# Eight GpSimd-issued transfers of x into a scratch tile, beside the loads of up and w_down

## The chip, the cores and the metric

The kernel runs on one core of one Trainium2 chip. The metric is the device time of a run in microseconds (us). Before the change the median of three runs is 411.18 us, with 411.07 and 411.40 at the ends.

A core has five engines that run their own instruction streams: TensorE (PE; its weight loads are shown as PEld), VectorE (DVE), ScalarE (ACT), GpSimd (POOL) and SyncE (SP). SP, ACT and POOL can issue transfers between the chip's memory (HBM) and the core's working memory (SBUF). A transfer is cut into packets, and these run on the core's 16 DMA engines. Each transfer counts up a semaphore as its parts land; instructions that need the data wait for the count.

## What is computed

One token is decoded through an attention block with a key and value cache and through a gated feed-forward block. Cut to what matters:

```python
# x (1,1,1024); k_cache, v_cache (1,4,65536,128); wq (1024,4096); wo (4096,1024)
# w_gate, w_up (1024,3584); w_down (3584,1024); all bf16
q = layernorm(x) @ wq                     # 32 heads of 128, 8 for each of the 4 cached heads
p = softmax(q @ k.T * 128**-0.5)          # over 65536 positions
h = x + (p @ v) @ wo
n = layernorm(h)
h2 = h + (gelu(n @ w_gate) * (n @ w_up)) @ w_down
```

Nearly all of the work is reading: 173.02 MB of weights and cache pass through the core once.

## The kernel before

**The ring and the order of loads.** All large inputs go through one SBUF buffer, `ring`, of four slots; `chunk()` hands out the next slot or slots. SP issues every large load in program order: wq (line 100), the cache (line 236, in `load`), wo (line 399), gate and up (line 441, in `ffn_in`) and w_down (line 497). A load waits until the matmuls (or, for k, the transposes) that read the slot's former contents are done. SP also issues ten small transfers (`c_dma`, line 395) of single rows of w_down into a tile `c_sb`, two after each large load from wo on.

**Attention.** For each of the four cached heads, `k_chunk` transposes k on DVE into tiles of the pool `ktpool` (tag "kt", six buffers) and multiplies on PE (line 257); the softmax runs on DVE and ACT; `v_chunk` multiplies the probabilities with v (line 306). The tail of this part multiplies with wo (line 404) and makes `h_col`, the columns of h (line 419).

**The feed-forward part.** `layernorm_cols` normalises h; GpSimd computes one step of it (line 159). `ffn_in` is called for gate and then for up: two loads each, 64 matmuls each (line 177), and a transpose of the result on DVE into a "kt" tile (line 189). Between the two calls the kernel prepares what the last product needs:

- `d_ps`, the accumulator of the output, is set to zero, and h is added into it by matmuls (line 472) that read the tile `hb`. GpSimd makes `hb`: a memset (line 467) and four copies from `h_col` (line 469).
- `actz`, a zeroed tile for the gated activations, is set by GpSimd (line 476); after up, DVE writes the activations into it (line 478).

Then `down` multiplies with w_down (line 484), which comes in four loads of 4096, 1792, 768 and 256 KB, and the result is copied (line 505) and stored by two transfers, one issued by SP (line 507) and one by ACT (line 508).

**What sets the order.** A scheduling layer records the operations and puts them into each engine's stream, with waits on semaphores between engines; a tile of a pool is given a buffer in turn, and its first writer waits for the last user of that buffer. At the end of the program SP waits for the completion counts of all transfers, two counts in an instruction, and then all engines meet in a barrier (the profile gives these instructions line 534). GpSimd issues no transfer in the kernel before.

Of the kernel before, what the change touches and what calls it, by code (L numbers as in the profile page):

```python
# [11 lines left out]
BF16 = mybir.dt.bfloat16  # L12
# [5 lines left out]
def kernel(  # L18
# [13 lines left out]
    nc = tc.nc  # L32
    P = 128
    D = A_x.shape[-1]
# [31 lines left out]
    ktpool = ctx.enter_context(tc.tile_pool(name="ktpool", bufs=6))  # L66
# [9 lines left out]
    def chunk(n=1):  # L76

        s0 = next_slot[0]
        assert s0 + n <= NSL
        next_slot[0] = (s0 + n) % NSL  # L80
        return ring[:, s0 * CW:(s0 + n) * CW]
# [91 lines left out]
    def wide_rows(banks, rows_z, ci, blocks, first, last):  # L173

        for t, w in enumerate(blocks):
            q = t % 4
            nc.tensor.matmul(banks[t // 4][32 * q:32 * q + 32, :], lhsT=rows_z[:, ci, :], rhs=w, start=first, stop=last,  # L177
                             tile_position=(0, 32 * q))

    def bank_pair(name, widths):  # L180
        return [ps_qk.tile([P, w], F32, name=name, tag="qk") for w in widths]

    def rows_to_columns(banks, name):

        w = [ps.shape[-1] for ps in banks]
        r = ktpool.tile([P, sum(w)], F32, name=name, tag="kt")
        o = 0
        for ps, n in zip(banks, w):
            nc.vector.transpose(out=r[:, o:o + n], in_=ps[:])  # L189
            o += n  # L190
        return r[:, 0:o:32]
# [200 lines left out]
    def c_dma():  # L392
        for _ in range(2):
            dst, src = c_loads.pop(0)
            nc.sync.dma_start(out=dst, in_=src)
# [32 lines left out]
    def f_blocks(w_row):  # L428

        blocks = []  # L430
        for o, n in zip((0, P * FA), FW):
            blocks += [w_row[:, o + q * n:o + (q + 1) * n].rearrange("k (j e) -> k e j", j=32) for q in range(4)]
        return blocks

    def ffn_in(wmat, name):
        banks = bank_pair(name + "_w", FW)
        wv_all = wmat.rearrange("(t p c) n -> t p c n", p=P, c=C4)
        for t in range(DS):
            w_sb = chunk()
            wv = w_sb[:, 0:C4 * F].rearrange("p (c n) -> p c n", c=C4)  # L440
            nc.sync.dma_start(out=wv, in_=wv_all[t])
            c_dma()
            for cc in range(C4):
                ci = t * C4 + cc
                wide_rows(banks, hz, ci, f_blocks(wv[:, cc, :]), ci == 0, ci == DC - 1)
        return rows_to_columns(banks, name + "_r")
# [21 lines left out]
    for i in range(4):  # L468
        nc.gpsimd.tensor_copy(out=hb[32 * i:32 * (i + 1), :, orow[i]:P:64],
                              in_=h_col[32 * i:32 * (i + 1), :].rearrange("p (t c) -> p c t", c=C4))  # L470
# [3 lines left out]
    AZ = 31  # L474
    actz = ptpool.tile([P, FC, 2 * AZ + 2], BF16, name="actz", tag="pt")
    nc.gpsimd.memset(actz[:], 0.0)
    u_r = ffn_in(B_w_up, "u_ps")
    nc.vector.tensor_tensor(out=actz[:, :, AZ], in0=u_r, in1=gl[:], op=ALU.mult)

# [59 lines left out]
```

## Time and profile before

| What | Value |
|---|---|
| Median of three runs | 411.18 us (411.07 to 411.40) |
| The profiled execution | 410.94 us, its span 409.0 us |
| Read from HBM | 173.02 MB, 423 GB/s over the span |
| PE busy | 243.9 us (60% of the span) |
| DVE busy | 204.7 us (50%) |
| ACT busy | 36.3 us (9%) |
| POOL busy | 35.9 us (9%), 119 instructions |
| Chain that ended last, by share | DMA 68%, DVE 22%, PE 5% |

The span runs from the first to the last instruction of the program in the profiled execution; the time of that execution is 1.94 us longer than the span. The profile page also cuts the span into 40 slices of 10.2 us and gives each engine's busy tenths; the chain of work that ended last is followed back from the last instruction, at each step to what released it. In the page's groups and in the timeline a line reads: engine, source line, operation, output<-input, shape and number.

The places named by their time are these: the last value loads are waited for from 288 us on, the wo product starts at 355.20 us, `h_col` is ready at 363 us, the gate product runs from 366.60 us, the up product in two halves from 380.75 and 389.27 us, the w_down product from 399.24 us, and the last store is issued at 406.67 us.

### The profile page before, as it was taken

What the parts mean: (1) busy time and instruction counts of PE and PEld (TensorE: products, weight loads), DVE (VectorE), ACT (ScalarE), POOL (GpSimd) and SP (SyncE); (2) the same over time, 40 slices, a digit from 0 to 9 for tenths busy, and PEclk for the clock granted to TensorE, in tenths of its full rate; (3) what the DMA queues carried; (4) which work ended last, traced back from release to release, by engine and by line L of the source; (5) the groups of instructions that cost most, each with busy time, mean ns of one, the idle gap of its engine ahead of it and who ended that gap; (6) DMA issues with size and microseconds to landing.
All of it is one profiled execution on the core that took longest, in us unless ns stands there. A gap on an engine that the chain in (4) does not pass through costs nothing.

```text
span 409.0 us, 3954 instructions
## 1 busy us (share of the span) xinstructions
PE 243.9 (60%) x1625; PEld 98.2 (24%) x1625; DVE 204.7 (50%) x262; ACT 36.3 (9%) x135; POOL 35.9 (9%) x119
## 2 busy tenths in 40 slices
PE   1337677688387457845765674677461423269865
PEld 1112222232132222311222221222130112131115
DVE  2118999999299339905980795099500000010210
ACT  1000000070000620000008000000340000000000
POOL 8223000300000400000002100000100100010000
PEclk9956988989889688866996888668885658588988
DMA  8999999999999999999999999999999999999995
GB/s 359 410 458 413 439 433 421 445 415 445 423 453 429 411 441 458 423 404 431 469 417 418 433 465 394 428 468 429 436 412 462 429 429 425 404 434 425 436 411 210
DMA packets 5441, 173.26 MB, mean 424 GB/s; under 512 B 688, under 2 KB 688, under 8 KB 1072
## 3 DMA queue, kind: packets, MB, share of 16 engines
q1 hardware_dynamic: 5368, 173.02, 98.4%
q8 instruction: 12, 0.20, 0.2%
q14 instruction: 5, 0.04, 0.0%
q10 hardware_dynamic: 56, 0.00, 0.0%
HBM read 173.02 MB, written 0.00 MB: 423 GB/s over the span
## 4 chain that ended last, share of the span: by engine, by line
DMA 68%; DVE 22%; PE 5%; issue 4%; SPq 0%
DMA ring<-in_A_k_cache_dram 42%; DVE kt L253 20%; DMA ring<-in_A_wo_dram 8%; DMA ring<-in_A_v_cache_dram 7%; DMA ring<-in_B_w_down_dram 6%; DMA ring<-in_B_w_up_dram 5%; PE qk_ps L257 2%; PE acc_ps L306 2%; DVE sc L267 1%; DVE mx L268 1%; PE at_ps L404 1%; SPq L100 0%; SPq L497 0%; PE d_ps L484 0%; DVE h L505 0%
## 5 line engine op out<-in xcount | busy, mean ns | idle before, releaser
L257 PE MATMUL qk_ps<-kt,qs 128*128 128x512 bf16 x512 | 141.3, 427 | 59.9 <-DVE kt L253 56.7
L253 DVE STREAM_TRANSPOSE kt<-ring 128x1024 f32<-128x1024 f32 x128 | 146.1, 1207 | 46.8 <-DMA ring<-in_A_k_cache_dram 46.8
L257 PEld LDWEIGHTS <-qs 128*128 128x128 bf16 x512 | 53.6, 105 | 144.4 <-issue 95.4
L306 PE MATMUL acc_ps<-ring,pt 128*32 128x512 bf16 x512 | 43.9, 519 | 48.2 <-DMA ring<-in_A_v_cache_dram 48.2
L290 ACT ACTIVATE pt<-sc,nbias 128x256 bf16<-128x256 f32 x64 | 31.5, 494 | 263.2 <-DVE nbias L283 263.2
L306 PEld LDWEIGHTS <-pt 128*32 128x32 bf16 x512 | 18.2, 126 | 72.3 <-issue 48.8
L324 DVE TENSOR_TENSOR oT_all<-o_ps,rl 128x8 bf16<-128x8 f32 x4 | 0.7, 167 | 45.1 <-PE o_ps L322 45.1
L267 DVE STREAM_TRANSPOSE sc<-qk_ps 128x512 f32<-128x512 f32 x32 | 22.1, 691 | 1.1 <-PE qk_ps L257 1.1
L268 DVE TENSOR_REDUCE mx<-sc 128x8 f32<-128x512 f32 x32 | 22.0, 688 | 1.1
L212 POOL MEMSET qs<- 128x2048 bf16 x4 | 7.2, 1804 | 94.5 <-PE qk_ps L257 94.5
L177 PEld LDWEIGHTS <-xz 128*32 128x32 bf16 x192 | 6.7, 123 | 35.1 <-issue 30.5
L177 PE MATMUL u_ps_w<-ring,xz 128*32 128x512 bf16 (+1 forms) x64 | 13.1, 974 | 2.2 <-DMA ring<-in_B_w_up_dram 2.2
L177 PE MATMUL g_ps_w<-ring,xz 128*32 128x512 bf16 (+1 forms) x64 | 12.9, 976 | 1.4 <-DVE xz L160 1.4
L404 PE MATMUL at_ps<-ring,o2z 128*32 128x512 bf16 x64 | 5.2, 493 | 12.6 <-DMA ring<-in_A_wo_dram 12.6
L216 POOL COPY qs<-qsel 32x32 bf16<-32x32 bf16 x64 | 11.2, 248 | 16.2 <-DVE qsel L207 15.5
L177 PE MATMUL qw_ps<-ring,xz 128*32 128x512 bf16 x64 | 7.2, 626 | 8.9 <-DMA ring<-in_A_wq_dram 8.9
L314 DVE TENSOR_TENSOR lsum<-lpart 128x8 f32<-128x8 f32 x4 | 0.7, 164 | 22.9 <-ACT pt L290 22.9
L290 ACT ACTIVATION_READ_ACCUMULATOR pt<-sc,nbias 128x1 f32 x64 | 12.0, 187 | 0.0
L419 DVE TENSOR_TENSOR h_col<-hc_ps,x_col 128x8 f32<-128x8 f32 x1 | 0.2, 167 | 20.3 <-PE hc_ps L412 20.3
L189 DVE STREAM_TRANSPOSE u_ps_r<-u_ps_w 128x512 f32<-128x512 f32 (+1 forms) x2 | 1.3, 650 | 13.8 <-PE u_ps_w L177 13.8
L189 DVE STREAM_TRANSPOSE q_r<-qw_ps 128x512 f32<-128x512 f32 x2 | 1.3, 696 | 13.1 <-PE qw_ps L177 13.1
L189 DVE STREAM_TRANSPOSE g_ps_r<-g_ps_w 128x512 f32<-128x512 f32 (+1 forms) x2 | 1.2, 650 | 12.4 <-PE g_ps_w L177 12.4
(94 smaller groups left out, 77.1 us busy)
## 6 DMA issues: line engine op xcount, KB each, us to landing
ring<-in_A_k_cache_dram SPq DMA_DIRECT2D x16, 4096.0 KB
ring<-in_A_wq_dram SPq DMA_DIRECT2D x2, 4096.0 KB
ring<-in_A_v_cache_dram SPq DMA_DIRECT2D x2, 4096.0 KB
ring<-in_B_w_gate_dram SPq DMA_DIRECT2D x2, 3584.0 KB
ring<-in_B_w_up_dram SPq DMA_DIRECT2D x2, 3584.0 KB
ring<-in_B_w_down_dram SPq DMA_DIRECT2D x1, 4096.0 KB
ring<-in_B_w_down_dram SPq DMA_DIRECT2D x1, 1792.0 KB
ring<-in_B_w_down_dram SPq DMA_DIRECT2D x1, 768.0 KB
```

The source lines that it names most:

```text
L177: nc.tensor.matmul(banks[t // 4][32 * q:32 * q + 32, :], lhsT=rows_z[:, ci, :], rhs=w, start=first, stop=last, tile_position=(0, 32 * q))
L189: nc.vector.transpose(out=r[:, o:o + n], in_=ps[:])
L212: nc.gpsimd.memset(qs[:], 0.0)
L216: nc.gpsimd.tensor_copy(out=qs[rows, :, s, SQ * i + s:SQ * (i + 1):NS], in_=qsel[rows, :, g * rep:(g + 1) * rep])
L253: nc.vector.transpose(out=kt[:], in_=k32[:, s * W:(s + 1) * W])
L257: nc.tensor.matmul(qk[:], lhsT=st["qs"][:, jt, s, :], rhs=mv[:, :, J, :, t], start=(s == 0 and jt == 0), stop=(s == NS - 1 and jt == 3))
L267: nc.vector.transpose(out=sc.rearrange("p n h s -> p (n h s)"), in_=qk[:])
L268: nc.vector.tensor_reduce(out=st["mx"][:, :, ci], in_=sc.rearrange("p n h s -> p h n s"), axis=AX.XY, op=ALU.max)
L290: nc.scalar.activation(out=pt[:].rearrange("p c n h s -> p (c n) h s")[:, :, r, :], in_=sc[:].rearrange("p c n h s -> p (c n) h s")[:, :, ...
L306: nc.tensor.matmul(acc[32 * c:32 * c + 32, :], lhsT=pt[:, ci % CPH, n, :, :].rearrange("p h s -> p (h s)"), rhs=v_sb[:, n:CH:NN, :], start ...
L314: nc.vector.tensor_tensor(out=lsum[:], in0=st["lpart"][:, 0, :], in1=st["lpart"][:, 1, :], op=ALU.add)
L404: nc.tensor.matmul(at_ps[32 * q:32 * q + 32, :], lhsT=o2z[:, c, :], rhs=wv[:, c, s * NB:(s + 1) * NB], start=(c < 2), stop=(c >= Hq - 2), ...
```

## The change

Between the zeroing of `actz` and the call of `ffn_in` for up, a scratch tile `marks` of 4 partitions x 8 x 256 elements (bf16) is taken from `ktpool`, and GpSimd issues eight transfers into it. Each reads all of x (1024 elements, 2 KB) as four rows of 256 elements, 512 bytes a row, into its own eighth of the tile. No instruction reads `marks`. The lines below the insertion are numbered five higher in the changed kernel.

```diff
     actz = ptpool.tile([P, FC, 2 * AZ + 2], BF16, name="actz", tag="pt")
     nc.gpsimd.memset(actz[:], 0.0)
+
+    NM = 8
+    marks = ktpool.tile([4, NM, D // 4], BF16, name="marks", tag="kt")
+    for i in range(NM):
+        nc.gpsimd.dma_start(out=marks[:, i, :], in_=A_x[0, 0].rearrange("(a b) -> a b", a=4))
     u_r = ffn_in(B_w_up, "u_ps")
     nc.vector.tensor_tensor(out=actz[:, :, AZ], in0=u_r, in1=gl[:], op=ALU.mult)
```

In the built program the first of the eight stands in GpSimd's stream between the memset of `hb` (line 467) and the copies into it (line 469); the other seven stand after those copies and are GpSimd's last work. None of the eight waits for a semaphore. On SP the closing waits become nine where there were five, since eight more completion counts are waited for; the count of SP's own output transfer stands in the second of the nine, where it stood in the third of the five. PE, DVE and ACT have the same instructions and waits as before.

## The prediction

> **What bounds the kernel now.** I read the page's DMA parts first, because the change adds transfers. In the second part of the page the DMA row gives, for 40 slices of the span, the busy share of the 16 DMA engines in tenths. In the third part the columns are packets, MB and the share of 16 engines' span.
>
> ```profile
> DMA  8999999999999999999999999999999999999995
> q1 hardware_dynamic: 5368, 173.02, 98.4%
> q8 instruction: 12, 0.20, 0.2%
> q14 instruction: 5, 0.04, 0.0%
> q10 hardware_dynamic: 56, 0.00, 0.0%
> ```
>
> The load queue (q1, issued by SP) fills the engines from the first slice to the last. q10 is the ACT queue (the load of x at line 95 and half of the output); q8 and q14 fetch instructions. Next, the end of the chain of work that ended last (start, duration, what):
>
> ```profile
> 358.42 22.29 DMA ring<-in_B_w_up_dram
> ...
> 381.22 24.73 DMA ring<-in_B_w_down_dram
> 405.96 0.04 issue
> 406.00 0.32 PE d_ps L484 x8
> 406.32 0.02 issue
> 406.34 0.29 DVE h L505
> ```
>
> The last 47 us are waits for loads; after the last load only 0.32 us of PE, 0.29 us of DVE, the two output transfers and the closing waits are left. In the trace's records of single DMA packets, joined end to start, every engine passes from one load packet to the next without a hole: the only holes over 0.2 us in 403 us are those in which an instruction fetch runs. So whatever engine time is added after 366 us delays the last load by as much, on the engines that finish last. How early the others finish is seen in the table of stretches (stretch, its length, busy time and instructions of PE, PEld, DVE, ACT, POOL, clock, DMA share, GB/s):
>
> ```profile
> 389.30:399.20 9.90, 6.78 (x36) 1.25 (x36) 1.74 (x4) 0.00 (x0) 0.00 (x0) 0.84 0.99 421
> 399.20:403.50 4.30, 4.04 (x160) 3.90 (x160) 0.00 (x0) 0.00 (x0) 0.00 (x0) 0.60 0.90 375
> 403.50:406.00 2.50, 1.49 (x81) 1.19 (x80) 0.00 (x0) 0.00 (x0) 0.00 (x0) 1.00 0.33 125
> ```
>
> The rate falls from 421 to 125 GB/s because engines run out of work one after the other. The 16 completions of the last load (256 KB of w_down) land from 402.72 to 405.96 us; the last five at 405.49, 405.66, 405.87, 405.93 and 405.96. A loss on an early engine is free up to its lead, at most 3.24 us; a loss shared by all is paid in full.
>
> **The change, part by part.** Nothing is removed. Added are eight transfers issued by GpSimd, each four rows of 512 bytes, 2 KB. No instruction reads `marks`, its "kt" buffer was freed long before, and in the built program PE, DVE and ACT keep the same instructions with the same waits. What differs is on POOL and SP.
>
> *POOL.* The first transfer stands between the memset of `hb` (L467) and the four copies into it (L469), the other seven after the copies. From the timeline:
>
> ```profile
> 365.98 0.53 POOL L467 MEMSET hb<- 128x512 f32 x1
> 366.57 0.89 POOL L469 COPY hb<-h_col 32x8 f32<-32x8 f32 x4
> ...
> 379.48 1.08 PE L472 MATMUL d_ps<-sel,hb 128*128 128x32 f32 x8
> ```
>
> The copies end at 367.46 and their reader starts at 379.48: 12.0 us of cover. No row shows a GpSimd issue. From below I bound it by an issue on SP (0.31 us, L507), from above by POOL's longest instruction (3.52 us, the memset of `c_sb`). Even at 3.52 us the copies end near 371 us, and all eight issues, 28.2 us, near 396 us, with nothing queued behind them until the program's end. Cost on POOL: 0 at both ends. If the first issue took over 12.0 us, the d_ps matmuls would be late, and past about 2 us more (PE waited 1.98 us for the second half of up at 389.27) the up matmuls too.
>
> *SP's closing waits.* SP closes the program by waiting for all completion counts, two in an instruction:
>
> ```profile
> L534 SPq EVENT_SEMAPHORE  x7: 17/28/889, 407.0 to 408.9; - x7
> ```
>
> Here the 889 ns one is the wait for SP's own output transfer, the third of five such waits; it ends at 408.05. The starts around it (407.03, 407.10, 407.17, then 408.09, 408.15, 408.22, 408.28) lie 61 to 69 ns apart. The built program has nine waits instead of five, and the one for that transfer is now second, so seven stand behind it where two stood: five more, 5 x 0.064 = 0.32 us, after the last transfer and hidden by nothing. I take +0.32; both ends are close (0.31 to 0.35).
>
> *Engine time of the added packets.* The nearest rows in kind and size are the ACT queue's load of the same x, early in the kernel beside full load traffic (the window from 3.6 to 6.5 us of the DMA view):
>
> ```profile
> q1 hardware_dynamic: 47, 1.54, 123.0%
> q10 hardware_dynamic: 47, 0.00, 0.9%
> ```
>
> In the packet records a 64-byte packet takes 8 to 11 ns, a 4-byte completion 9 ns, a 256-byte one 16 to 18 ns, and a 2,048-byte one 84 ns; along that line 512 bytes take about 27 ns. If the 32 rows are spread evenly, an engine gets two, 54 ns; with at most eight completions, 72 ns: 0.06 to 0.13 us per engine. I take 0.12.
>
> *Changing queues.* This is the unknown. In those rows a load packet of 32,768 bytes after a q10 packet takes 1,213 to 1,224 ns, as anywhere else (median 1,214): changing to ACT's queue and back costs nothing. From below, then, 0. The other rows of a foreign queue are the instruction fetches. A q14 packet of 8,192 bytes takes 309 to 325 ns, which is its bytes' time, but the load packet after it on that engine is longer by 312, 661, 380, 661 and 414 ns; after the q8 packets of 16,384 bytes (982 to 1,107 ns) it is longer by 467 to 550 ns. The size hardly matters, so I read it as a fixed price of 0.31 to 0.66 us, mean 0.49, for coming back from such a queue. From above, every visit costs 0.66 us. An engine gets between 2 visits (the rows alone, evenly spread) and 8 (each transfer touches every engine), so 0 to 5.3 us. The GpSimd queue is neither an SP nor an ACT queue; of the two I put a row-carrying visit nearest to the fetches, whose packets too come from another place of memory on a queue that neither SP nor ACT feeds, and a bare completion nearest to q10's 9 ns. Two visits x 0.49 = 0.98 us.
>
> The Trainium skill, page "DMA: Bandwidth & Descriptors", section "Why a DMA increments its semaphore by 16 and not by 1", says that a GpSimd-issued transfer has all 16 engines post a completion, whatever its shape; no row here shows it. By that rule each engine is visited eight times, and with the same return price the sum would be 8 x 0.49 + 0.32 + 0.12 = 4.4 us in place of the one below.
>
> **Sum.** 0.32 + 0.12 + 0.98 = 1.42 us (with 0.31 and 0.66 a visit: 1.06 to 1.76). The profiled execution took 410.94 us (span 409.0 and 1.94 us around it) and would become 412.36; the median of the runs is 411.18, so 412.6, its own range 412.2 to 412.9.
>
> **The rivals.**
> 1. *Hidden (not slower).* The visits cost as little as those to ACT's queue. Place: the load stream from 366 to about 396 us; price 0.12 us of packets plus 0.32 of closing waits; it decides if the return price is below 0.2 us (0.44 + 2 x 0.19 = 0.82 us is the bound of what can be told). For it: the q10 rows are the same source and nearly the same size, and the queue is read by the same engines. Against it: q10 is fed as SP's queue is, and the only rows of another kind all show a loss. Time 411.6.
> 2. *Every completion is a visit.* All 16 engines lose 0.31 to 0.66 us eight times: 2.5 to 5.3 us plus 0.44. For it: the price didn't depend on size. Against it: q10's completions cost 9 ns, and close visits could share one return. At 0.49: 415.5; at 0.31: 414.1. The rows all falling on the same four engines would come near it too, if those are among the last to finish; if they are early ones, their lead of up to 3.24 us takes it up.
> 3. *GpSimd's first transfer is slow and hb becomes late.* It decides above 14 us (12.0 of cover and 2 of PE's wait). No row on POOL is longer than 3.52 us. At 20 us: about 6 + 0.4, 417.6.
> 4. *Faster.* The fetches move with the instruction counts (POOL has eight transfers more), and one of them, 16,384 bytes at 403.57, lies in the tail. It occupies one engine for 1.07 us; but with completions at 405.93 and 405.96, freeing one engine gains 0.03 us alone. A gain of over 0.82 us would need several of the last engines relieved at once, up to 1.07 us: 410.1. I see no row for that.
>
> **How the numbers follow.** Forecast 0.37, hidden 0.30, every completion 0.23, slow first transfer 0.03, faster 0.07. About 0.2%, 0.82 us here, is what a measurement of this kernel can tell from no change; the forecast, the second and the third rival lie beyond it, slower 0.63; hidden is within it, 0.30; faster 0.07. The predicted time is the forecast's, 412.6. The range takes in the hidden case (411.6, less 0.2 for the spread of the runs before) and the second rival at 0.49 a visit: 411.4 to 415.5. Outside are the faster case, the slow first transfer and the dear end of the second rival.
>
> **What would show it.** In the new profile a further DMA queue stands with 32 rows and 32 to 128 completions, of about 9 and 27 ns. If the forecast holds, load packets of 28,672 bytes between 366 and 396 us that follow a row of the new queue take about 1.4 to 1.7 us instead of 1.07, two per engine, and the piece of w_down in the chain ends near 407.1. If rival 1 holds, none is longer and the last load lands near 406.1; if rival 2 does, some eight per engine are, and it lands near 410. L534 on SP should have eleven waits, seven of them behind that for the output, 0.45 us where two took 0.13. The copies into `hb` should end before 372 us; later than 379 would speak for rival 3. A new queue that makes the engines wait without longer packets, or a time around the span that differs from 1.94 us, would make the working wrong.

## The result, and the profile after

The changed kernel takes 411.76 us (median of 18 runs, 411.37 to 412.15) against 411.22 us (18 runs, 410.85 to 411.40) for the kernel before in the same measurement: ratio 1.0014, 95% interval 1.0008 to 1.0021. It is slower by 0.54 us. The interval lies above 1, and the difference below the 0.82 us that the prediction took as the bound and below the forecast's 1.42 us. The profiled execution took 411.37 us, its span 409.45 us.

The DMA parts of the changed kernel's page (busy tenths in 40 slices; queue, packets, MB, share of 16 engines):

```profile
DMA  8999999999999999999999998999999999999994
q1 hardware_dynamic: 5368, 173.02, 98.3%
q8 instruction: 12, 0.20, 0.2%
q0 software_dynamic: 256, 0.02, 0.0%
q14 instruction: 5, 0.04, 0.0%
q10 hardware_dynamic: 56, 0.00, 0.0%
```

q0 is the new queue. It carries 256 packets, not the 64 to 160 that were foreseen, and still takes 0.0% of the engines' time; the load queue keeps its packets, and the engines stay full. The end of the chain of waits of the changed kernel (start, duration, what):

```profile
358.09 22.94 DMA ring<-in_B_w_up_dram
...
381.54 24.67 DMA ring<-in_B_w_down_dram
406.21 0.04 issue
406.25 0.32 PE d_ps L489 x8
406.57 0.02 issue
406.60 0.29 DVE h L510
```

The path is the same. The last load lands at 406.21 us where it landed at 405.96, 0.25 later, and the two steps behind it are unchanged. The table of stretches of the changed kernel, with the columns of the one shown of before:

```profile
399.20:403.50 4.30, 3.77 (x160) 3.54 (x160) 0.00 (x0) 0.00 (x0) 0.00 (x0) 0.66 0.94 389
403.50:406.00 2.50, 1.34 (x80) 1.19 (x80) 0.00 (x0) 0.00 (x0) 0.00 (x0) 1.00 0.36 142
```

A little more traffic is left for the last 2.5 us: 142 GB/s instead of 125. In the records of completions, the last five of the last load come at 405.65, 405.71, 405.84, 405.86 and 406.21 us: four by 405.86, earlier than the last two before, and one engine alone late.

On GpSimd, the timeline of the changed kernel (start, duration, engine, line, operation):

```profile
365.73 0.52 POOL L467 MEMSET hb<- 128x512 f32 x1
366.20 0.71 POOL L481 DMA_DIRECT2D marks<-in_A_x_dram  x1
366.91 0.93 POOL L469 COPY hb<-h_col 32x8 f32<-32x8 f32 x4
367.77 3.58 POOL L481 DMA_DIRECT2D marks<-in_A_x_dram  x7
...
379.30 1.08 PE L472 MATMUL d_ps<-sel,hb 128*128 128x32 f32 x8
```

An issue costs GpSimd 0.52 us, the first 0.71. The copies into `hb` end at 367.84; their reader starts at 379.30. The rest of the view of the tile `marks` says when the data came:

```profile
L481 POOL DMA_DIRECT2D marks<-in_A_x_dram x8: 518/518/713, 366.2 to 370.8; - x8
...
DMA to landing us min/median/max: 6.6/11.0/15.8
```

The eight transfers of 2 KB took 6.6 to 15.8 us to land: they wait in the engines, not at GpSimd. Last, the closing line of the program, 539 now (engine, operation, count: shortest, median, longest ns, first and last start):

```profile
L539 SPq EVENT_SEMAPHORE  x11: 17/28/28, 407.3 to 409.4; - x11
...
L539 POOLq EVENT_SEMAPHORE_RANGE_CLEAR  x1: 139/139/139, 409.0 to 409.0; - x1
```

There are eleven waits where there were seven. SP's wait for its own output passes at 408.11 us; the seven behind it start at 408.18 to 408.55 us, 59 to 67 ns apart. Clearing the semaphores takes 139 ns where it took 96.

**The account of the profiled execution.** The last load is 0.25 us later. From the landing of SP's output to the end of the span it is 1.35 us instead of 0.95: +0.40, of which five more waits are 0.31 and GpSimd's longer drains and clearing about 0.07. SP's output itself landed in 1.18 us instead of 1.37: -0.19. The sum is 0.46, and the span grew by 0.47. The -0.19 does not go with the change: which of the two outputs lands first differs from profile to profile. SP's took 1.18 us in after and e5 and 1.19 in e8, where it was first, and 1.35 to 1.37 in before, e1, e4 and e6, where it was second.

### The profile page after: what moved, and what is told of

Same layout as the page of the kernel before. It is cut to its first block, busy times and chain, and to the rows that moved or that the text cites. A ratio compares the mean times of both kernels' runs of the same rounds, so it can differ in the third digit from the quotient of the medians.

```text
span 409.4 us, 3966 instructions
## 1 busy us (share of the span) xinstructions
PE 245.2 (60%) x1625; PEld 98.6 (24%) x1625; DVE 204.8 (50%) x262; ACT 36.3 (9%) x135; POOL 40.0 (10%) x127
## 4 chain that ended last, share of the span: by engine, by line
DMA 68%; DVE 22%; PE 5%; issue 4%; SPq 0%
DMA ring<-in_A_k_cache_dram 42%; DVE kt L253 19%; DMA ring<-in_A_wo_dram 8%; DMA ring<-in_A_v_cache_dram 7%; DMA ring<-in_B_w_down_dram 6%; DMA ring<-in_B_w_up_dram 6%; PE qk_ps L257 2%; PE acc_ps L306 1%; DVE sc L267 1%; DVE mx L268 1%; PE at_ps L404 1%; SPq L100 0%; SPq L502 0%; PE d_ps L489 0%; DVE h L510 0%
## 5 line engine op out<-in xcount | busy, mean ns | idle before, releaser
L257 PE MATMUL qk_ps<-kt,qs 128*128 128x512 bf16 x512 | 143.0, 432 | 57.5 <-DVE kt L253 48.6
```

Of the source, the lines that this page charges most:

```text
L257: nc.tensor.matmul(qk[:], lhsT=st["qs"][:, jt, s, :], rhs=mv[:, :, J, :, t], start=(s == 0 and jt == 0), stop=(s == NS - 1 and jt == 3))
```

## The experiments

Two questions stood open. How much of the 0.54 us is the closing waits and how much the load stream? And why did a foreign packet not cost what an instruction fetch costs: is it its size, its number, or the engines that it falls on? Differences below are against the runs of the kernel before that were taken with the experiment. For the endings, this table of profiled executions is used (us):

| Profile | last load lands | mean of its 16 completions | end of span | from the last landing to the end | median against before |
|---|---|---|---|---|---|
| before | 405.96 | 404.53 | 408.98 | 3.02 | |
| e8_shift_before | 405.97 | 404.51 | 408.96 | 2.99 | -0.17 |
| after | 406.21 | 404.69 | 409.45 | 3.24 | +0.54 |
| e5_after_again | 406.73 | 404.75 | 409.97 | 3.24 | +0.62 |
| e4_shift_after | 406.31 | 404.75 | 409.31 | 3.00 | +0.33 |
| e1_one32 | 406.35 | 404.70 | 409.49 | 3.14 | +0.37 |
| e6_late32 | 406.49 | 405.00 | 409.90 | 3.41 | +0.80 |

**The same kernel again (e5_after_again).** The changed kernel without an edit.

> The changed kernel as it is, timed on the same chip and against the same runs as the next three. Its profile had SP's closing waits and the clearing of counts at 0.38 us more than before, and all rows of the added transfers on four DMA engines, eight on each. Theory V (closing part 0.39; on those four engines eight rows of 27 ns and eight completions of 9 ns, 0.29): +0.4 to +0.7 us. If the first measurement was drawn low and the load stream loses as much as the runs with one transfer seemed to show (0.25 us on top): +0.8.

Measured 411.73 us (11 runs, 411.55 to 412.00) against 411.11: ratio 1.0014, interval 1.0005 to 1.0023. The 0.5 to 0.6 us stand. Its chain of waits:

```profile
382.05 24.69 DMA ring<-in_B_w_down_dram
406.73 0.04 issue
```

The load ends 0.52 us later than in the first profile of the same kernel, while the ending is 3.24 us in both. The last landing is the part that varies from one execution to the next (406.21, 406.31 and 406.73 us in the three profiles with these eight transfers), and a single profile can't place it better. The mean of the 16 completions is steadier: 404.53 and 404.51 us in the two profiles without the transfers, 404.69 to 404.75 in the three with them. By it the load stream loses 0.17 to 0.24 us on the average engine. The new queue's packets take 0.18 us an engine by their records.

**The closing waits moved (e4_shift_after, e8_shift_before).** One small load into `c_sb` is left out (8 of the 3,584 rows of w_down are then not multiplied). The counts are given out in turn, so both outputs move to the last two of them, and the other waits pass before the outputs land.

```diff
-    c_loads.append((c_sb[33:62:4, 2:3, :], c_views[3]))
...
-        for _ in range(2):
+        for _ in range(min(2, len(c_loads))):
```

e4 makes this edit in the changed kernel:

> The changed kernel without the last small load of w_down rows (8 rows of 2 KB; these 8 of the 3,584 rows of w_down are left out of the product), which shifts the completion counts by one: the two output transfers now use the last two counts waited for, so all other closing waits pass before the outputs land. Theory W: against the changed kernel 7 waits x 0.064 = 0.45 less and 0.09 less engine time: 411.76 - 0.54 = 411.2. If the closing waits cost nothing (the time is all lost in the load stream): 411.76 - 0.09 = 411.67.

Measured 411.38 us (411.07 to 411.72) against 411.05: +0.33, ratio 1.0008, interval 0.9999 to 1.0016. The closing line of this kernel:

```profile
L538 SPq EVENT_SEMAPHORE  x11: 17/28/28, 407.4 to 409.2; - x11
```

It still has eleven waits, but seven of them pass from 407.38 to 407.79 us, before the outputs land at 408.20 and 408.38. From the last landing to the end it is 0.93 us, as in the kernel before (0.95), and the ending of the table falls to 3.00. In the profile the waits cost by their place behind the outputs, not by their number. The median lies between the two cases named beforehand (no difference from the kernel before, or 0.45 us if the waits cost nothing), and its interval takes in both. e8 makes the same edit in the kernel before:

> The kernel before without the last small load of w_down rows (8 of the 3,584 rows are left out of the product), so that the two outputs use the last two completion counts waited for. Theory V: two waits less behind the output's landing, 0.13, and 0.09 us less on eight engines: -0.1 to -0.2 us, 410.9 to 411.0. It is the partner of the changed kernel with the same load left out: between the two only the engine time (0.29) and the longer clearing (0.07) remain, 0.36, where between the changed kernel and the one before there were 0.54.

Measured 410.94 us (410.55 to 411.27) against 411.11: -0.17, ratio 0.9994, interval 0.9985 to 1.0003; its ending is 2.99 us. So with the order of the closing waits equal, the eight transfers cost 0.33 + 0.17 = 0.50 us by the medians, where I had expected about 0.36, and with intervals of about 0.7 us on both medians the one is not told from the other. By the medians the shift is worth 0.21 to 0.29 us in the changed kernel and 0.17 in the kernel before, so the five added waits would come to 0.04 to 0.12 us; that neither confirms nor excludes the 0.31 of the profile. What is told apart is the ending: 3.24, 3.24 and (e6) 3.41 with seven waits behind the outputs, 3.00, 2.99, 3.02 without.

**One transfer instead of eight (e1_one32).** The same number of bytes in 32 rows, from wq, in one transfer: one count to wait for.

```diff
-    marks = ktpool.tile([4, NM, D // 4], BF16, name="marks", tag="kt")
-    for i in range(NM):
-        nc.gpsimd.dma_start(out=marks[:, i, :], in_=A_x[0, 0].rearrange("(a b) -> a b", a=4))
+    marks = ktpool.tile([32, D // 4], BF16, name="marks", tag="kt")
+    nc.gpsimd.dma_start(out=marks[:], in_=A_wq[0:32, 0:D // 4])
```

> One GpSimd transfer of 32 rows of 512 bytes (from wq) in place of eight of four rows: the same 16 KB and 32 rows, but one completion count instead of eight. Theory W (the 0.54 us is SP's closing waits, 0.32, the longer clearing of counts and drains on GpSimd at the end, 0.07, and 18 packets per engine, 14 of 9 ns and 2 of 27 ns, 0.18): here six closing waits with three behind the output's instead of two, 0.06, and two rows and a few completions per engine, 0.07 to 0.09: 411.22 + 0.15 = 411.37. Theory R (the rows themselves cost the load stream, 0.25 us each and two per engine): 411.7. Theory S (whatever it is, it is per transfer, 0.07 us each, in the load stream): 411.3. Load packets of 28,672 bytes stay at 1,066 ns under W and S, some are over 1,250 under R.

Measured 411.42 us (411.12 to 411.64) against 411.05: +0.37, ratio 1.0008, interval 0.9999 to 1.0017. From its page and from its chain:

```profile
q0 software_dynamic: 32, 0.02, 0.0%
```

```profile
381.66 24.69 DMA ring<-in_B_w_down_dram
406.35 0.04 issue
```

From SP's output to the end it is 1.08 us, 0.13 more than before: one more wait behind it (0.064) and GpSimd's part. The load stream did not get off free: the 32 packets are 16 of 1,024 bytes (two rows in one, 54 ns), one on every engine, and 16 of 4 bytes. The load packets behind the rows are longer by 0.05 to 0.09 us on all engines (one, on an engine that had just run an instruction fetch, by 0.41), neither unchanged nor over 1.25 us long, as the theories had it. Load packets that ran at that time without a row in front are longer too, by up to 0.07. In all that is about 0.085 us an engine, so each engine pays 0.054 + 0.085 + 0.009 = 0.15 us; the mean of the 16 completions is 0.17 later. 0.13 + 0.15 is 0.28 of the 0.37. I had left this lengthening out.

**Long rows (e3_rows8k, e7_spread8k).** If the price of a visit is fixed, rows of 8,192 bytes, the size of a q14 fetch, cost no more beyond their own time. e3 keeps eight transfers of four rows. The tile comes from the pool of `sc`, whose buffers are free earlier, so that GpSimd issues them at 298 to 305 us, beside the loads of v, whose packets are 65,536 bytes.

```diff
-    marks = ktpool.tile([4, NM, D // 4], BF16, name="marks", tag="kt")
+    marks = scpool.tile([4 * NM, HD], BF16, name="marks", tag="sc")
...
-        nc.gpsimd.dma_start(out=marks[:, i, :], in_=A_x[0, 0].rearrange("(a b) -> a b", a=4))
+        nc.gpsimd.dma_start(out=marks[4 * i:4 * i + 4, :], in_=A_wq[4 * i:4 * i + 4, :])
```

> The eight transfers with rows of 8,192 bytes (of wq) instead of 512, the size of the instruction fetches that made the next load packet 0.31 to 0.66 us longer. Theory W with price by bytes: two rows per engine at 0.31 us each instead of 0.027, so 0.57 us more than the changed kernel: 412.3. If the longer next packet comes with the size of a foreign packet (the price that the prediction put on a visit, but by size): 2 x 0.49 more, 413.3, and load packets behind such rows are 0.3 to 0.66 us longer in the trace. If it belongs to the fetch queues alone: 412.3 and no longer packets.

Measured 416.47 us (416.27 to 416.52) against 411.05: ratio 1.0129, interval 1.0114 to 1.0145. Its chain:

```profile
386.39 24.71 DMA ring<-in_B_w_down_dram
411.10 0.04 issue
```

That is 3 us above the dearest case named beforehand. The last load lands 5.14 us later than before, but the 16 completions of that load spread from 403.05 to 411.10 us: twelve come by 407.64, four from 409.93 on. In the packet records a row takes 0.32 us in the mean (309 to 512 ns) and the load packet behind it is longer by about 0.25 us in the mean (0.83 at most), and all 32 rows are on four engines, eight on each: 8 x (0.32 + 0.25) = 4.6 us there. The other twelve are late too: their completions have a mean of 405.23 us, against 404.53 for all 16 before. e7 spreads the same rows: two transfers of 16.

```diff
-    NM = 8
+    NM = 2
...
-        nc.gpsimd.dma_start(out=marks[4 * i:4 * i + 4, :], in_=A_wq[4 * i:4 * i + 4, :])
+        nc.gpsimd.dma_start(out=marks[16 * i:16 * i + 16, :], in_=A_wq[16 * i:16 * i + 16, :])
```

> The same 32 rows of 8,192 bytes as in the run with eight transfers of four rows, but in two transfers of 16 rows over 16 partitions, issued at the same place. Theory V (the four-row transfers put all their rows on the same four engines, eight rows each, 0.32 us a row and 0.24 on the next load packet, which is the 5.4 us of that run): with 16 rows a transfer every engine gets two rows: 2 x 0.56 = 1.1, closing part 0.2: +1.3 us, 412.4. If the cost comes with the bytes or rows in total, wherever they run: +5 us, 416. If a load packet behind such a row is longer by 0.49, the price of the prediction: 2 x 0.81 + 0.2 = 1.8.

Measured 414.18 us (414.00 to 414.63) against 411.11: ratio 1.0074, interval 1.0061 to 1.0086. Its chain:

```profile
384.54 24.75 DMA ring<-in_B_w_down_dram
409.28 0.04 issue
```

The place of the rows matters: two rows on every engine cost 2.3 us less than eight on four. But 16 such rows run at once, take 0.41 us each in the mean, and the load packet behind is longer by 0.75 us in the mean (0.08 to 1.2), so an engine pays 2 x (0.41 + 0.75) = 2.3 us on average, where I had counted with e3's price. The mean of the 16 completions is 3.04 us later than before, so 0.7 us stay outside this sum.

The packet records show where these 0.7 us lie, and they change the reading. Load packets that follow no row, but run while a row is read on another engine, are longer too: by 10 to 11 us in sum over the 16 engines in either kernel, 0.7 us an engine. In e7 the first row starts at 302.03 us, and nine load packets that had started 0.8 to 1.6 us earlier are already longer by 0.31 to 1.1 us. In the kernel before, only the load packets behind the two instruction fetches are long beside the loads of v. So the loss with these rows is not only a price on the packet behind: it falls on load packets of all engines. What causes it stays open. The rows of e1, e3 and e7 come from wq and those of the changed kernel and e6 from x, so the size of a row is not told apart from its source; e3 and e7 differ in how many rows run at once and on which engines.

**Four times as many transfers (e2_mid32, e6_late32).** To ask for a price by the transfer, 32 transfers of four 128-byte rows go into a constant tile in the middle of the cache loads.

```diff
+    NM = 32
+    marks = const.tile([P, 2, 64], BF16, name="marks")
+
+    def mark(i):
+        nc.gpsimd.dma_start(out=marks[4 * (i // 2):4 * (i // 2) + 4, i % 2, :],
+                            in_=A_x[0, 0].rearrange("(a b) -> a b", a=16)[0:4, :])
...
             k_chunk(g, ci)
+            if g == Hkv - 1 and ci == 0:
+                for i in range(NM):
+                    mark(i)
```

> 32 GpSimd transfers of four rows of 128 bytes of x, issued in the attention part after the last qs tile (about 140 us on) instead of eight in the tail; eight completion counts are used in turn, so the closing waits are nine as in the changed kernel. Theory W: closing waits 0.32, clearing 0.07, and 32 x 2 packets per engine of 9 ns (eight of them rows, some 12 ns): 0.60; together 0.99, 412.2. The engine time counts although it falls 150 us ahead of the end. Theory S (0.07 us per transfer in the load stream): 32 x 0.07 = 2.2, 413.5. If the place matters and time lost in the attention part is won back: 0.39, 411.6.

Measured 438.61 us (438.23 to 439.25): ratio 1.0671, interval 1.0656 to 1.0686, far from what was expected, and for a reason outside the question. Nothing in the program holds these transfers back, so the scheduler put them at the start of GpSimd's stream. Its timeline:

```profile
12.68 4.29 POOL L331 DMA_DIRECT2D marks<-in_A_x_dram  x8
20.45 0.52 POOL L331 DMA_DIRECT2D marks<-in_A_x_dram  x1 [3.48 <-DMA marks<-in_A_x_dram]
...
63.22 2.05 POOL L331 DMA_DIRECT2D marks<-in_A_x_dram  x4 [0.75 <-DMA marks<-in_A_x_dram]
65.27 5.91 POOL L216 COPY qs<-qsel 32x32 bf16<-32x32 bf16 x32
```

The first eight go out without a wait; the next twenty each wait for an earlier one to land, and the last four go out after one more wait (in brackets: the idle time before it and what ended it). GpSimd's transfers use eight completion counts in turn, so these are waits of the program for a count to be free. The copies into `qs` stand behind all of them and start at 65.27 us; in the kernel before they start at 28.27. The matmuls with the cache wait for them, and the loads for the matmuls:

```profile
PEld L257 <- POOL qs L216: 40.2, 2, 39.9
```

```profile
DMA  8999952698888999999999999999999999999995
```

The first is a line of the table of waits (40.2 us in two waits), the second the page's DMA row: the engines run dry in slices 6 to 8. This is the third rival's mechanism in a place without cover. e6 holds the transfers with a copy that writes `marks` from the last head's `qs`:

```diff
+                nc.gpsimd.tensor_copy(out=marks[:].rearrange("p a b -> p (a b)"), in_=kst[g]["qs"][:, 0, 0, :])
```

> 32 GpSimd transfers of four rows of 128 bytes, held back by a copy from the last qs tile, so that no work of the attention part stands behind them on GpSimd; eight completion counts in turn, nine closing waits. Theory V: closing part 0.39; the four engines with the rows get 32 x (13 + 9) ns = 0.70: 1.1 us in all, 412.2. Rows spread over all engines: 64 packets of 9 to 13 ns on each, 0.6: 1.0 us (not told apart by the time, but by the trace). If each visit made the next load packet longer, by 0.02 us on average as behind the 512-byte rows: 0.64 more on the four engines, 1.7 us. If time lost in the attention part is won back: 0.4.

Measured 411.91 us (411.66 to 412.18) against 411.11: +0.80, ratio 1.0018, interval 1.0010 to 1.0027. From its page and the view of its tile:

```profile
q0 software_dynamic: 1024, 0.02, 0.1%
```

```profile
L331 POOL DMA_DIRECT2D marks<-in_A_x_dram x32: 521/521/713, 139.3 to 214.7; - x32
...
DMA to landing us min/median/max: 6.8/21.9/27.9
```

That is under the 1.1 us expected. 32 transfers and 1,024 packets cost 0.2 us more than eight and 256, and SP's output to the end is 1.35 us as in the changed kernel. There is no price by the transfer worth naming: but for those that meet an instruction fetch, load packets behind a 128-byte row or behind 4 bytes are longer by less than 0.01 us in the mean.

## Why the prediction was right or wrong

**The direction and the range were right; the likeliest case was not the one that came.** The time is the first rival's: 411.6 foreseen, 411.76 measured, with its condition (a return price below 0.2 us) met. The forecast's own range, 412.2 to 412.9, missed; the stated range holds the time because it took in that rival.

**GpSimd: right.** Costed at nothing behind 12.0 us of cover. The first issue took 0.71 us of it and the other seven 3.58 us behind the copies. e2 shows what GpSimd's issues can cost without cover: 27.5 us for 32 of them and their waits.

**SP's closing waits: right by the profile.** Foreseen 0.32 us, seven waits behind the output taking 0.45; the trace has five more at 0.059 to 0.067 us, 0.31 in all, seven taking 0.435. GpSimd's drains and clearing, 0.07, were not in the sum. e4, where the same waits pass before the outputs land, has its ending back at 3.00 us; the medians are too wide to confirm it.

**Packet time: near, from wrong counts.** Foreseen 0.12 us on every engine, two rows and at most eight completions. In the joined records of load and q0 packets the rows were on four engines only, eight each, and every transfer put two packets on all 16 engines (a row and a completion, or two of 4 bytes). On the four engines that is 8 x 0.027 + 8 x 0.009 = 0.29 us, on the others 16 x 0.009 = 0.14.

**The return price: the step that failed.** The term "Two visits x 0.49 = 0.98 us" was mis-sized. A load packet behind a 512-byte row is longer by 0.014 us in the mean and 0.16 at most; behind 4 bytes, away from instruction fetches, by less than 0.005 in the mean. So two visits gave 0.03 us and eight on an engine 0.11, where 0.98 was foreseen. The step put the new queue nearest to the instruction fetches and read their loss as fixed, because 8,192 and 16,384 bytes cost alike; but the foreign packets at hand below that, q10's, had cost nothing. In the other runs the load packet behind was longer by about 0.07 us for 1,024 bytes, 0.25 for 8,192 on four engines and 0.75 for 8,192 on 16 at once. That size is the cause is not shown: those longer rows came from wq, and load packets without a row in front were longer beside them too. But a fixed price is excluded, and two sizes near each other do not show that size is without weight. Why an instruction fetch costs 0.31 to 0.66 us stays open. What is true of the step: not every visit is free. One of the four engines gathered 0.34 to 0.52 us of lengthening in each of the traces of after, e4 and e5, most of it behind rows and some behind 4 bytes (in after 38, 55, 62, 28, 61, 29, 87 and 159 ns). Whether this engine is the one that lands last is not shown, and why the other three have 0.1 us at most is open.

**The sum.** In place of 0.32 + 0.12 + 0.98 stand 0.2 to 0.4 for the ending (0.40 less what the output's landing happens to give back) and, by the mean of the completions, 0.17 to 0.24 for the load stream. Together that is 0.4 to 0.64, and 0.54 and 0.62 were measured. The last landing itself can't give the split: it varies by more than the term between two profiles of the same kernel.

**The rivals.** Every completion a visit fell: every engine had 16 packets of the new queue and not eight, and one of 4 bytes lengthened the next load packet by less than 0.005 us in the mean. Its last case, all rows on the same four engines, did come, but eight rows on an engine brought it 0.29 us of packets and 0.11 of lengthening in the mean, and not eight times 0.31 to 0.66. The slow first transfer fell for this place. Faster did not come: the lead of the early engines was there, but nothing relieved the last ones.

**The signs named beforehand.** 32 rows as foreseen, but 224 packets of 4 bytes instead of 32 to 128. No load packet behind a row is at 1.4 to 1.7 us (the longest is 1.07 + 0.16; those of 1.48 to 1.59 us in this stretch follow instruction fetches). The piece of w_down ended at 406.21, by the first rival's 406.1 and not the forecast's 407.1. The time around the span is 1.92 us.

## What to carry to other kernels

A few small transfers beside a saturated load stream cost here about their own packets on the engines that they fell on; ask which engines those are, and make their rows small or spread them, for rows of 8,192 bytes on four engines cost ten times as much (5.4 us), and spread over all of them 3.1. Each completion count that transfers use is also waited for at the end of the program, at 0.064 us for two counts, and in the profiles it costs only if the wait stands behind the last output's. And a transfer that nothing holds is put wherever the scheduler likes: look at what stands behind it on its engine, since in e2 and e6, after eight in flight, the issue itself waited for a landing.

## What the runs showed of the hardware that was not expected

- A GpSimd transfer of four rows puts two packets on each of the 16 engines: 32 packets per transfer, 256 in all. The Trainium skill, page "DMA: Bandwidth & Descriptors", section "Why a DMA increments its semaphore by 16 and not by 1", says that all 16 engines post a completion whatever the shape; the trace agrees.
- The rows of all eight transfers lie on the same four engines, and so do those of e3 and e6. The same section lets a transfer of four shares take consecutive engines from a cursor that goes round; no such turning is seen in these traces, and the measurement decides. (The records do not number the engines, so whether the four are neighbours is not seen.)
- An engine serves one packet of the new queue between two packets of the load queue, most of them 1.07 us long, so the 16 packets of each engine are spread over 370.0 to 386.1 us, and a transfer of 2 KB took up to 15.8 us to land. Beside the cache loads of e6, whose packets are longer, a transfer of 512 bytes took up to 27.9 us.
